# Attention and a four-expert MoE in float32: the first expert product in three float32r passes, the second without its seven-product scheme

## The chip, the cores and the metric

The kernel runs on one NeuronCore of one Trainium2 chip. Its time is what the device needs for one execution, in microseconds; the figure given is the median of the runs. A profile is one execution, recorded by the hardware; its span goes from the first to the last instruction.

The engines by their names in the profile: PE is TensorE (matmuls), PEld its weight loads, ACT is ScalarE, DVE is VectorE, POOL is GpSimd, SP issues the DMAs. Each takes its instructions in the order in which they were put down, and waits for semaphores of the others.

## The reference

Polynomial-sketch attention on inputs of 4 batches x 4 heads x 1088 tokens x 32, whose output, 4352 tokens of 128 numbers, is the input `x` of a mixture of four experts:

```python
p = domain_probs / (domain_probs.sum(-1, keepdims=True) + 1e-09)   # (4352, 4)
out = np.zeros((N, D), dtype=np.float32)                           # (4352, 128)
for e in range(E):                                                 # 4 experts
    h = np.maximum(x @ w1[e], 0.0)                                 # w1[e]: (128, 1024)
    out += p[:, e:e + 1] * (h @ w2[e])                             # w2[e]: (1024, 128)
return out.astype(np.float32)
```

All of it is float32. The two expert products are nearly all of the arithmetic.

## The kernel before, in words

The tokens, transposed so that the 128 features are the partitions (`xT`), are cut into eleven chunks of 128, 448, six times 512, 320, 256 and 128 columns (`CHUNKS`). The first and the last chunk are "plain" and are done with tokens as output partitions. Every chunk goes through `NQ` = 16 steps: 4 experts `e` times 4 pairs of 128-wide blocks of the hidden layer (`f`), two blocks `j` in each step. The main loop walks `i` over all steps of all chunks and calls `first(i, work)`, then `second(i - LA)` with `LA` = 2: the second product runs two steps behind the first.

- `first`, before: for each block `j` a float32 product of 128x128 weights with the chunk's columns, issued by `both` as two column halves of 64 (`on_side` alternates them, line 202), into a bank of pool `ps_h`. ScalarE rectifies it into `hid` (line 817), and VectorE's `rectify_and_subtract` (line 786) makes the combinations of half chunks that the seven-product scheme needs.
- `second`, before: seven products of 64 output rows and half a chunk's columns in place of eight, with weights from `w2_sb` and from their sums `w2s` (made once on GpSimd by `weight_sums`), accumulated over the expert's four steps in two banks, `o0` and `o1`, with one buffer each.
- `gather(m, e)`, after an expert's last `second`: two ScalarE copies of the accumulators into `ev` (lines 920 and 921), then, in the generator `gather_rest`, sums on GpSimd, two copies that move 64 partitions (933, 934), the multiplication with the gates and the sum over the experts in `total`. `turn_back` transposes the total and stores it.
- `work` issues pieces of the attention of later tokens (`front`: `keys`, `queries`, `attend`) between these steps, as many as the coming chunks need; all of the attention's matmuls are 64 columns wide (`on_side`).
- SP carries every load and store in one queue: batches of q, k, v (`load_batch`), the gates (`store_gates`, `load_gate`), the way of the attention's output through DRAM (`xd`) into `xT`, and the output.

The order on each engine is the order in which these Python calls put instructions down (`manual_schedule`). PSUM has eight banks of 512 float32 columns; before, three belong to `ps_h`, two to `ps_o`, one to `ps_f`, two to `ps_n`.

What follows an expert's last second product, before (in `gather`, an ordinary function, called in the main loop):

```python
nc.scalar.copy(_ap(ev, 0, P, 0, [[2 * w, 2], [1, w]]), _ap(a0, 0, P, 0, two))
nc.scalar.copy(_ap(ev, 0, P, w, [[2 * w, 2], [1, w]]), _ap(a1, 0, P, 0, two))
...
return gather_rest(m, e, ev, yz)
```

and the loop's end, which the change leaves as it is:

```python
second(i - LA)
mm, kk = steps[i - LA]
if kk % NP == NP - 1 and not plain(mm):
    ending = chain(ending, gather(mm, kk // NP))
else:
    next(ending, None)
```

Of the kernel before, what the change touches and what calls it, by code (L numbers as in the profile page):

```python
# [9 lines left out]
BF16 = mybir.dt.bfloat16  # L10
I32 = mybir.dt.int32
# [12 lines left out]
def kernel(  # L24
# [52 lines left out]
    ps_h = ctx.enter_context(tc.tile_pool(name="ps_h", bufs=3, space=bass.MemoryType.PSUM))  # L77
# [10 lines left out]
    def load_rows(src, b, name, part=slice(0, S)):  # L88

        d = kn if name == "kn" else qn  # L90
        if b not in d:
            d[b] = lpool.tile([P, S], F32, tag=name, bufs=2, name=name)
        c, n = part.start, part.stop - part.start
        base = src.offset + b * H * S * D
        if name == "qn" and b == B - 1:
            for c, n, t in ((0, (G - 4) * D, 0), ((G - 4) * D, 4 * D, S - P)):
                nc.sync.dma_start(d[b][:, c : c + n], bass.AP(src.tensor, base + t * D, [[S * D, H], [n, 32], [1, n]]))
        else:
            nc.sync.dma_start(d[b][:, part], bass.AP(src.tensor, base + c, [[G * D, P], [1, n]]))
# [163 lines left out]
    gates = dram.tile([B, GE * 32], F32, name="gates")  # L263
# [28 lines left out]
    def store_gates():  # L292
        nc.vector.transpose(pt[:, :], pn[:, :])
        for b in range(B):
            nc.sync.dma_start(
                gates[b].rearrange("(x r j) -> r x j", r=32, j=32),
                pt[32 * b : 32 * b + 32, :].rearrange("r (x j) -> r x j", j=32),
            )
# [11 lines left out]
    def load_gate(m, engine=nc.sync):  # L310
        gate[m] = mpool.tile([P, CW * E], F32, tag="gate", name="gate")
        for b, c, n, at in parts(m):
            engine.dma_start(
                gate[m][:, at * E : (at + n) * E], gates[b, c * E : (c + n) * E].partition_broadcast(P)
            )
# [342 lines left out]
    w2s = cpool.tile([P, E, FB // 2, 4, HP], F32, name="w2s")  # L658

    def block(e, i, j):  # L660
        return _ap(w2_sb, 0, P, e * FB * DM + P * j + HP * i, [[2 * DM, FB // 2], [1, HP]])

    def weight_sums(e):
        s = [w2s[:, e, :, i, :] for i in range(4)]
        for out, in0, in1, op in (
            (s[0], block(e, 1, 0), block(e, 1, 1), ALU.add),
            (s[1], s[0], block(e, 0, 0), ALU.subtract),
            (s[2], block(e, 0, 0), block(e, 1, 0), ALU.subtract),
            (s[3], block(e, 0, 1), s[1], ALU.subtract),
        ):  # L670
            nc.gpsimd.tensor_tensor(out=out, in0=in0, in1=in1, op=op)
            yield

    def start():
# [9 lines left out]
        for gi in range(3):  # L684
            kf.append(psum(ps_h, "h"))
# [7 lines left out]
        fq = [psum(ps_o, "o0"), psum(ps_o, "o1"), psum(ps_n, "num")]  # L693
# [26 lines left out]
        qT = apool.tile([P, QW], F32, tag="qT2", name="qT2")  # L720
# [7 lines left out]
        early[b, n] = psum(ps_o, "o1")  # L728
# [26 lines left out]
    def gate_of(m, e):  # L755
        return _ap(gate[m], 0, P, 32 * e, [[32 * E, CHUNKS[m] // 32], [1, 32]])

    def by_blocks(t, n, off=0):
        return _ap(t, 0, P, off, [[32, n // 32], [1, 32]])

# [14 lines left out]
    def first(i, work):  # L775
# [5 lines left out]
        w = n // 2  # L781
        hd = mpool.tile([P, 4 * CW], F32, tag="hid", bufs=4, name="hid")
        hid[i] = hd

        def rectify_and_subtract(out, src, in1):
            nc.vector.scalar_tensor_tensor(out=out, in0=src, scalar=0.0, in1=in1, op0=ALU.max, op1=ALU.subtract)  # L786

        if plain(m):
            if i in begun_hp:
# [22 lines left out]
            return  # L812
        for j in range(2):
            hp = psum(ps_h, "h")
            c = P * (2 * f + j)
            both(hp[:, 0:n], w1_sb[:, e, c : c + P], xT[:, START[m] : START[m] + n], start=True, stop=True)
            nc.scalar.activation(hd[:, n * j : n * j + n], hp[:, 0:n], ACTF.Relu)  # L817
            if j == 0:
                rectify_and_subtract(hd[:, 4 * w : 5 * w], hp[:, w:n], hd[:, 0:w])
            else:  # L820
                rectify_and_subtract(
                    _ap(hd, 0, P, 5 * w, [[w, 2], [1, w]]),
                    _ap(hp, 0, P, w, [[0, 2], [1, w]]),
                    _ap(hd, 0, P, w, [[3 * w, 2], [1, w]]),
                )
                rectify_and_subtract(hd[:, 7 * w : 8 * w], hp[:, 0:w], hd[:, 6 * w : 7 * w])
            work()

    begun = [0, 0]

    def second(i):
# [3 lines left out]
        if plain(m):  # L835

            if f == 0:
                acc[m] = psum(ps_o, f"o{e % 2}")
# [24 lines left out]
        if f == 0:  # L863
            acc[m, e] = [psum(ps_o, "o0"), psum(ps_o, "o1")]
            begun[:] = [0, 0]
        w = n // 2
        blk = lambda a, j: w2_sb[:, e, 2 * f + j, HP * a : HP * a + HP]
        new = lambda a: w2s[:, e, f, a, :]
        place = lambda a: hd[:, w * a : w * a + w]

        todo = (
            [(blk(0, 0), place(0)), (new(3), place(3)), (blk(0, 1), place(2)), (new(1), place(6))],
            [(new(2), place(5)), (new(0), place(4)), (blk(1, 1), place(7)), (new(1), place(6))],
        )
        at = [0, 0]
        for _ in range(7):
            s = turn[0]
            p = at[s]
            at[s] += 1

            fresh = p >= begun[s]
            begun[s] = max(begun[s], p + 1)
            wt, mv = todo[s][p]
            on_side(
                lambda s: acc[m, e][p // 2][half[s], w * (p % 2) : w * (p % 2) + w],
                lambda s: wt,
                lambda s: mv,
                start=(fresh and p % 2 == 0),
                stop=(f == NP - 1),
                skip_group_check=True,  # L890
            )

    def turn_back(m, src):

        n = CHUNKS[m]
        ob = mpool.tile([P, CW], F32, tag="ob", name="ob")
# [12 lines left out]
    def gather(m, e):  # L909

        n = CHUNKS[m]
        w = n // 2
        a0, a1 = acc.pop((m, e))
        ev = mpool.tile([P, 2 * CW], F32, tag="ev", name="ev")
        two = [[w, 2], [1, w]]
        add = lambda out, in0, in1, op=ALU.add: nc.gpsimd.tensor_tensor(out=out, in0=in0, in1=in1, op=op)  # L918

        nc.scalar.copy(_ap(ev, 0, P, 0, [[2 * w, 2], [1, w]]), _ap(a0, 0, P, 0, two))  # L920
        nc.scalar.copy(_ap(ev, 0, P, w, [[2 * w, 2], [1, w]]), _ap(a1, 0, P, 0, two))  # L921
        yz = mpool.tile([P, 2, CW // 2], F32, tag="yz", bufs=1, name="yz")
        add(yz[:, :, 0:w], _ap(ev, 0, P, 0, [[2 * w, 2], [1, w]]), _ap(ev, 0, P, 3 * w, [[0, 2], [1, w]]))
        return gather_rest(m, e, ev, yz)

    def gather_rest(m, e, ev, yz):
        n = CHUNKS[m]
        w = n // 2
        two = [[w, 2], [1, w]]
        add = lambda out, in0, in1, op=ALU.add: nc.gpsimd.tensor_tensor(out=out, in0=in0, in1=in1, op=op)  # L930
        yield
        sh = mpool.tile([P, CW // 2], F32, tag="sh", bufs=1, name="sh")
        nc.scalar.copy(sh[HP:P, 0:w], yz[0:HP, 0, 0:w])  # L933
        nc.scalar.copy(sh[0:HP, 0:w], yz[HP:P, 1, 0:w])
        add(ev[HP:P, 0:w], yz[HP:P, 0, 0:w], sh[HP:P, 0:w])
        add(ev[0:HP, 2 * w : 3 * w], yz[0:HP, 1, 0:w], sh[0:HP, 0:w])
        ct = mpool.tile([P, CW], F32, tag="ct", bufs=1, name="ct")
        add(_ap(ct, 0, P, 0, two), _ap(ev, 0, P, 0, [[0, 2], [1, w]]), _ap(ev, 0, P, w, two))
        if e == 0:
            total[m] = mpool.tile([P, CW], F32, tag="total", name="total")  # L940
        add(by_blocks(ct if e else total[m], n), by_blocks(ct, n), gate_of(m, e), ALU.mult)
        if e:
            add(total[m][:, 0:n], total[m][:, 0:n], ct[:, 0:n])
# [9 lines left out]
    behind = cpool.tile([P, 1], F32, name="behind")  # L953
# [17 lines left out]
    for i in range(3):  # L971
        begun_hp[i] = psum(ps_h, "h")
        half_columns(i, begun_hp[i], 0)
    to_sum = chain.from_iterable(weight_sums(e) for e in range(E))
    ending = iter(())
    for i in range(len(steps) + LA):
        if i < len(steps):
# [16 lines left out]
            if i > NQ - 4:  # L994
                if i == NQ - 3:

                    nc.gpsimd.tensor_copy(behind[:, :], xT[:, START[2] - 1 : START[2]])
                next(to_sum, None)
            if i == 2:
                gate_quotients()  # L1000
            elif i == 5:
                store_gates()
                load_gate(1)
                load_gate(2)
                load_batch(1)
            if m > 1 and kq == LA + 3 and m + 2 < NC:
                load_gate(m + 1)
# [41 lines left out]
```

## Time and profile before

| | |
|---|---|
| median of 3 runs | 488.05 us (487.61 to 488.38) |
| span of the profiled execution | 485.9 us |
| median less span (what lies around it) | 2.15 us |
| PE busy | 481.5 us, 99% |
| DVE busy | 320.9 us, 66% |
| ACT busy | 246.8 us, 51% |
| POOL busy | 230.0 us, 47% |
| granted TensorE clock | 1.000 |

No other time of the profiled execution is recorded; the span is what the parts are summed against.

How to read the views: a group's line gives the source line, engine, operation, tiles (out<-in), shape (partitions x elements) and count, then the busy time in us, the mean of one in ns, the idle time of the engine before them, and what ended it. A float32 matmul is two records of PE, each with a weight load. A chain line gives start, length, engine, tile and line, and how many records were merged. A wait line reads "engine tile line <- who released it: us in total, times, longest".

### The profile page before, as it was taken

How to read it: one execution, taken by the hardware profiler on the slowest of the kernel's cores; microseconds unless marked ns; L12 is line 12 of the kernel's file. 1: busy time of each engine (PE TensorE's matmuls, PEld its weight loads, DVE VectorE, ACT ScalarE, POOL GpSimd, SP SyncE). 2: the span in 40 equal slices, each digit the busy share in tenths (PEclk: the TensorE clock that was granted, in tenths of full speed). 3: DMA queues.
4: the chain of work that ended last, by engine and by line, in shares of the span. 5: the costliest groups of instructions: out<-in, count | busy, mean ns of one | idle time of the engine just before them, and what ended most of it. 6: DMA issues, size and time to landing. Idle time of an engine off the chain costs nothing.

```text
span 485.9 us, 11377 instructions
## 1 busy us (share of the span) xinstructions
PE 481.5 (99%) x4551; PEld 362.7 (75%) x4551; DVE 320.9 (66%) x759; ACT 246.8 (51%) x496; POOL 230.0 (47%) x270
## 2 busy tenths in 40 slices
PE   8999999999999999999999999999999999999997
PEld 6965666667777777777777777677777777999997
DVE  6859675686766668486776757668684666665642
ACT  4354564445544555355445555445455555566651
POOL 5172654435444455415455444424555445555571
PEclk9999999999999999999999999999999999999999
DMA  7990050211003123031103100021101200120001
GB/s 223 278 299 10 23 150 12 88 20 45 2 9 106 24 69 93 2 89 20 40 1 130 24 12 1 3 86 24 34 0 56 50 1 0 45 55 4 15 1 20
DMA packets 37772, 26.25 MB, mean 54 GB/s; under 512 B 24824, under 2 KB 34520, under 8 KB 37208
## 3 DMA queue, kind: packets, MB, share of 16 engines
q1 hardware_dynamic: 37704, 25.53, 18.9%
q8 instruction: 36, 0.59, 0.5%
q14 instruction: 16, 0.13, 0.1%
q10 hardware_dynamic: 16, 0.00, 0.0%
HBM read 21.28 MB, written 4.24 MB: 53 GB/s over the span
## 4 chain that ended last, share of the span: by engine, by line
PE 97%; DMA 1%; DVE 1%; issue 0%; SPq 0%; ACT 0%; ACTq 0%
PE h L202 50%; PE o L202 41%; PE f L202 3%; PE den L202 2%; DMA kn<-in_k_dram 1%; PE num L202 1%; DVE qp L501 0%; DVE kp L391 0%; DVE kT L328 0%; DVE qT L488 0%; SPq L125 0%; DVE end L856 0%; DVE kvz L414 0%; ACT fs L360 0%; ACT vx L337 0%
## 5 line engine op out<-in xcount | busy, mean ns | idle before, releaser
L202 PE MATMUL h<-xT,w_sb 128*64 128x512 f32 (+5 forms) x1424 | 300.2, 491 | 0.0
L786 DVE SCALAR_TENSOR_TENSOR hid<-h,hid 128x256 f32<-128x256 f32 (+6 forms) x432 | 203.7, 472 | 143.3 <-ACT hid L817 134.9
L817 ACT ACTIVATE hid<-h 128x512 f32<-128x512 f32 (+3 forms) x288 | 158.5, 550 | 192.3 <-PE h L202 146.2
L202 PE MATMUL o<-hid,w2s 128*64 128x256 f32 (+3 forms) x1152 | 224.0, 355 | 0.0
L202 PEld LDWEIGHTS h<-xT,w_sb 128*64 128x64 f32 x1424 | 147.5, 137 | 50.4 <-issue 6.4
L202 PE MATMUL o<-hid,w_sb 128*64 128x256 f32 (+3 forms) x864 | 183.7, 355 | 0.0
L202 PEld LDWEIGHTS o<-hid,w2s 128*64 128x64 f32 x1152 | 132.2, 137 | 28.9
L930 POOL TENSOR_TENSOR ev<-yz,sh 64x256 f32<-64x256 f32 (+3 forms) x72 | 48.7, 676 | 159.9 <-ACT sh L933 157.2
L202 PEld LDWEIGHTS o<-hid,w_sb 128*64 128x64 f32 x864 | 100.5, 137 | 25.2 <-issue 5.8
L918 POOL TENSOR_TENSOR yz<-ev 128x512 f32<-128x512 f32 (+3 forms) x36 | 41.7, 1160 | 60.4 <-ACT ev L921 60.2
L930 POOL TENSOR_TENSOR ct<-ev 128x512 f32<-128x512 f32 (+3 forms) x36 | 42.5, 1182 | 2.8
L930 POOL TENSOR_TENSOR total<-total,ct 128x512 f32<-128x512 f32 (+3 forms) x27 | 31.9, 1181 | 2.1
L930 POOL TENSOR_TENSOR ct<-ct,gate 128x512 f32<-128x512 f32 (+3 forms) x27 | 31.8, 1177 | 2.1
L501 DVE TENSOR_TENSOR qp<-qa,qb 64x512 f32<-64x512 f32 (+5 forms) x44 | 30.1, 685 | 1.0
L920 ACT COPY ev<-o 128x512 f32<-128x512 f32 (+3 forms) x36 | 19.4, 539 | 12.7 <-PE o L202 12.3
L202 PE MATMUL o<-w_sb,hid 128*64 128x128 f32 x256 | 22.3, 273 | 0.0
L921 ACT COPY ev<-o 128x512 f32<-128x512 f32 (+3 forms) x36 | 19.4, 539 | 2.0
L202 PEld LDWEIGHTS o<-w_sb,hid 128*64 128x64 f32 x256 | 18.1, 137 | 1.6 <-issue 0.9
L809 ACT ACTIVATE hid<-h 128x256 f32<-128x256 f32 x23 | 8.4, 384 | 18.3 <-PE h L202 17.9
L391 DVE TENSOR_TENSOR kp<-fs 128x256 f32<-128x256 f32 (+1 forms) x24 | 16.6, 696 | 0.1
L933 ACT COPY sh<-yz 64x256 f32<-64x256 f32 (+3 forms) x36 | 13.7, 380 | 1.7 <-POOL yz L918 0.8
L202 PEld LDWEIGHTS den<-kvx,qp 128*64 128x64 f32 x240 | 12.5, 137 | 2.5 <-issue 0.5
(129 smaller groups left out, 247.5 us busy)
## 6 DMA issues: line engine op xcount, KB each, us to landing
w_sb<-in_moe_w_dram SPq DMA_DIRECT2D x8, 512.0 KB, 5.8
gate<-gates SPq DMA_DIRECT2D x4, 1024.0 KB, 4.7
kn<-in_k_dram SPq DMA_DIRECT2D x4, 544.0 KB, 7.0
vn<-in_v_dram SPq DMA_DIRECT2D x16, 128.0 KB, 3.5
gate<-gates SPq DMA_DIRECT2D x2, 896.0 KB, 6.4
qn<-in_q_dram SPq DMA_DIRECT2D x2, 544.0 KB, 4.0
out_dram<-ob SPq DMA_DIRECT2D x16, 64.0 KB, 2.0
qn<-in_q_dram SPq DMA_DIRECT2D x2, 480.0 KB, 5.0
```

The lines of the kernel that those rows point to most:

```text
L202: nc.tensor.matmul(out(s), weights(s), moving(s), **flags)
L391: eng.tensor_tensor(out=_ap(kps[b], 0, P, 256 * t0 + P * p + 64 * x, [[256, n], [32, 2], [R, 4], [1, R]]), in0=_ap(src, 0, P, off + 4 * x, ...
L501: nc.vector.tensor_tensor(out=qp[p][64 * x : 64 * x + 64, 0:n], in0=qa[64 * p : 64 * p + 64, 0:n], in1=qb[64 * p : 64 * p + 64, 0:n], op=A ...
L786: nc.vector.scalar_tensor_tensor(out=out, in0=src, scalar=0.0, in1=in1, op0=ALU.max, op1=ALU.subtract)
L809: nc.scalar.activation(hd[:, 0 : 2 * n], hp[:, 0 : 2 * n], ACTF.Relu)
L817: nc.scalar.activation(hd[:, n * j : n * j + n], hp[:, 0:n], ACTF.Relu)
L918: add = lambda out, in0, in1, op=ALU.add: nc.gpsimd.tensor_tensor(out=out, in0=in0, in1=in1, op=op)
L920: nc.scalar.copy(_ap(ev, 0, P, 0, [[2 * w, 2], [1, w]]), _ap(a0, 0, P, 0, two))
L921: nc.scalar.copy(_ap(ev, 0, P, w, [[2 * w, 2], [1, w]]), _ap(a1, 0, P, 0, two))
L930: add = lambda out, in0, in1, op=ALU.add: nc.gpsimd.tensor_tensor(out=out, in0=in0, in1=in1, op=op)
L933: nc.scalar.copy(sh[HP:P, 0:w], yz[0:HP, 0, 0:w])
```

## The change

`w1` and the tokens are cut into a high and a low piece of at most twelve bits each, scaled, with the difference of the two as a third: `wa`, `wb`, `wd` for the weights (ScalarE and VectorE, `weight_parts`, one piece of work per step from step 7 on), `xa`, `xb`, `xd` for the tokens (`token_parts`, at the last step of the chunk before). The product is then `wa xa + wb xb` in one bank and `wd xd` in another, as float32r matmuls on full 128x128 tiles; ScalarE copies the first out with a scale, VectorE subtracts the second from it, ScalarE rectifies the result in place, one block later. The second product is a plain float32 product on full tiles into one bank. `gather` has one copy and no sums over halves. The gates lie in DRAM by expert and are loaded by expert, in tiles of one chunk's columns.

The diff, cut to its core:

```diff
-    ps_h = ctx.enter_context(tc.tile_pool(name="ps_h", bufs=3, space=bass.MemoryType.PSUM))
+    ps_h = ctx.enter_context(tc.tile_pool(name="ps_h", bufs=2, space=bass.MemoryType.PSUM))
+    ps_g = ctx.enter_context(tc.tile_pool(name="ps_g", bufs=2, space=bass.MemoryType.PSUM))
     ps_o = ctx.enter_context(tc.tile_pool(name="ps_o", bufs=1, space=bass.MemoryType.PSUM))
...
+    def weight_parts(e):
+        HF = F // 2
+        for c in (slice(0, HF), slice(HF, F)):
+            nc.scalar.activation(wa[:, e, c], w1_sb[:, e, c], ACTF.Copy, scale=4096.0 * NEAR)
+            stt(wb[:, e, c], w1_sb[:, e, c], 4096.0, wa[:, e, c].bitcast(F32), ALU.subtract)
+            yield
+            stt(wd[:, e, c], wa[:, e, c].bitcast(F32), R12, wb[:, e, c].bitcast(F32), ALU.subtract)
+            yield
...
+    def token_parts(m):
...
+        nc.scalar.activation(xa[:, 0:n], x, ACTF.Copy, scale=R12 * NEAR)
+        stt(xb[:, 0:n], xa[:, 0:n].bitcast(F32), -4096.0, x, ALU.add)
+        nc.vector.tensor_tensor(
+            out=xd_[:, 0:n], in0=xa[:, 0:n].bitcast(F32), in1=xb[:, 0:n].bitcast(F32), op=ALU.subtract
+        )
...
         for j in range(2):                                   # in first()
-            hp = psum(ps_h, "h")
-            both(hp[:, 0:n], w1_sb[:, e, c : c + P], xT[:, START[m] : START[m] + n], start=True, stop=True)
-            nc.scalar.activation(hd[:, n * j : n * j + n], hp[:, 0:n], ACTF.Relu)
...
+            g1, g2 = psum(ps_h, "h"), psum(ps_g, "g")
+            nc.tensor.matmul(g1[:, 0:n], wa[:, e, c], xa, start=True, stop=False)
+            nc.tensor.matmul(g1[:, 0:n], wb[:, e, c], xb, start=False, stop=True)
+            nc.tensor.matmul(g2[:, 0:n], wd[:, e, c], xd_, start=True, stop=True)
+            out = hd[:, n * j : n * j + n]
+            nc.scalar.activation(out, g1[:, 0:n], ACTF.Copy, scale=1.0 + R12)
+            rectify()
+            nc.vector.tensor_tensor(out=out, in0=out, in1=g2[:, 0:n], op=ALU.subtract)
+            to_rectify.append(out)
             work()
...
+    def rectify():
+        while to_rectify:
+            out = to_rectify.pop(0)
+            nc.scalar.activation(out, out, ACTF.Relu)
...
         if f == 0:                                           # in second()
-            acc[m, e] = [psum(ps_o, "o0"), psum(ps_o, "o1")]
...
+            acc[m, e] = psum(ps_o, "o")
+        for j in range(2):
+            nc.tensor.matmul(
+                acc[m, e][:, 0:n],
+                w2_sb[:, e, 2 * f + j, :],
+                hd[:, n * j : n * j + n],
+                start=(f == j == 0),
+                stop=(f == NP - 1 and j == 1),
+            )
...
     def gather(m, e):
         n = CHUNKS[m]
...
-        return gather_rest(m, e, ev, yz)
...
+        ev = mpool.tile([P, CW], F32, tag="ev", bufs=1, name="ev")
+        nc.scalar.copy(ev[:, 0:n], acc.pop((m, e))[:, 0:n])
+        g = gate.pop((m, e))[:, 0:n]
         if e == 0:
             total[m] = mpool.tile([P, CW], F32, tag="total", name="total")
+            nc.gpsimd.tensor_tensor(out=total[m][:, 0:n], in0=ev[:, 0:n], in1=g, op=ALU.mult)
+        else:
+            nc.gpsimd.tensor_tensor(out=ev[:, 0:n], in0=ev[:, 0:n], in1=g, op=ALU.mult)
+            nc.gpsimd.tensor_tensor(out=total[m][:, 0:n], in0=total[m][:, 0:n], in1=ev[:, 0:n], op=ALU.add)
         yield
...
             first(i, work)                                   # in the main loop
-            if i > NQ - 4:
...
+            if i > NQ - 10:
+                next(to_part, None)
+            if kq == NQ - 1 and m + 2 < NC:
+                while have[0] < START[m + 1] + CHUNKS[m + 1]:
+                    piece()
+                token_parts(m + 1)
```

In the changed kernel's line numbers: `weight_parts` 679 with `stt` 673, `token_parts` 692 and 694, the three matmuls 833 to 835, the copy 837, the subtraction 839, the rectification 848, the second product 885, the copy in `gather` 913.

More of the change, by code (lines that the diff above doesn't have):

```diff
@@ L10 @@
 BF16 = mybir.dt.bfloat16
+F32R = mybir.dt.float32r
 I32 = mybir.dt.int32
@@ L91, in load_rows @@
         if b not in d:
-            d[b] = lpool.tile([P, S], F32, tag=name, bufs=2, name=name)
+            d[b] = lpool.tile([P, S], F32, tag=name, bufs=1 if name == "kn" else 2, name=name)
         c, n = part.start, part.stop - part.start
@@ L260 @@
     mask_a = [[4 * x + l // R for l in range(32)] for x in range(2)]
-    gates = dram.tile([B, GE * 32], F32, name="gates")
+    gates = dram.tile([B, E, GE * 32 // E], F32, name="gates")
     pn = cpool.tile([P, GE], F32, name="pn")
@@ L294, in store_gates @@
         for b in range(B):
[L295 to L298, printed above, removed]
+            for e in range(E):
+                p = list(pt.ap)[0][0]
+                nc.sync.dma_start(
+                    gates[b, e].rearrange("(x r j) -> r x j", r=32 // E, j=32),
+                    bass.AP(pt.tensor, pt.offset + (32 * b + e) * p, [[E * p, 32 // E], [32, GE // 32], [1, 32]]),
+                )
     def parts(m):
@@ L308, with load_gates @@
     gate = {}
[L310 to L315, printed above, removed]
+    def load_gates(m, experts):
+        for e in experts:
+            gate[m, e] = mpool.tile([P, CW], F32, tag="gate", bufs=6, name="gate")
+            for b, c, n, at in parts(m):
+                nc.sync.dma_start(gate[m, e][:, at : at + n], gates[b, e, c : c + n].partition_broadcast(P))
     xT = cpool.tile([P, B * S], F32, name="xT")
@@ L655, in queries, with stt @@
         yield from attend(b, c, n, qp)
[L658 to L671, printed above, removed]
-            yield
+    R12 = 2.0 ** -12
+    NEAR = 1.0 - 2.0 ** -13
+    wa = cpool.tile([P, E, F], F32R, name="wa")
+    wb = cpool.tile([P, E, F], F32R, name="wb")
+    wd = cpool.tile([P, E, F], F32R, name="wd")
+    def stt(out, in0, scalar, in1, op1):
+        nc.vector.scalar_tensor_tensor(out=out, in0=in0, scalar=scalar, in1=in1, op0=ALU.mult, op1=op1)
+    def weight_parts(e):
[3 more added lines that the diff above has]
+            stt(wb[:, e, c], w1_sb[:, e, c], 4096.0, wa[:, e, c].bitcast(F32), ALU.subtract)
+            yield
+            stt(wd[:, e, c], wa[:, e, c].bitcast(F32), R12, wb[:, e, c].bitcast(F32), ALU.subtract)
+            yield
+    xparts = {}
+    def token_parts(m):
+        n = CHUNKS[m]
+        xa, xb, xd_ = (mpool.tile([P, CW], F32R, tag=f"x{i}", name=f"x{i}") for i in "abd")
+        x = xT[:, START[m] : START[m] + n]
+        nc.scalar.activation(xa[:, 0:n], x, ACTF.Copy, scale=R12 * NEAR)
[3 more added lines that the diff above has]
+        )
+        xparts[m] = xa, xb, xd_
     def start():
@@ L684, in start @@
         for gi in range(3):
-            kf.append(psum(ps_h, "h"))
+            kf.append(psum(ps_h, "h") if gi < 2 else psum(ps_g, "g"))
         value = value_copy(b)
@@ L692, in start @@
             pass
-        fq = [psum(ps_o, "o0"), psum(ps_o, "o1"), psum(ps_n, "num")]
+        fq = [psum(ps_o, "o"), psum(ps_g, "g"), psum(ps_n, "num")]
         for i in range(3):
@@ L719, in start @@
         n1 = UNITS[b][1]
-        qT = apool.tile([P, QW], F32, tag="qT2", name="qT2")
+        qT = apool.tile([P, QW], F32, tag="y", name="qT2")
         turns = query_turns(b, n, n1, qT)
@@ L727, in start @@
         next(first)
-        early[b, n] = psum(ps_o, "o1")
+        early[b, n] = psum(ps_g, "g")
         both(early[b, n][:, 0:n1], sq[:, :], qT[:, 0:n1], start=True, stop=True)
@@ L753, in plain @@
         return m in (0, NC - 1)
[L755 to L759, printed above, removed]
     begun_hp, made_hp = {}, {}
@@ L780, in first @@
         n, (e, f) = CHUNKS[m], divmod(kq, NP)
-        w = n // 2
-        hd = mpool.tile([P, 4 * CW], F32, tag="hid", bufs=4, name="hid")
+        hd = mpool.tile([P, 2 * CW], F32, tag="hid", bufs=3, name="hid")
         hid[i] = hd
-        def rectify_and_subtract(out, src, in1):
-            nc.vector.scalar_tensor_tensor(out=out, in0=src, scalar=0.0, in1=in1, op0=ALU.max, op1=ALU.subtract)
         if plain(m):
+            rectify()
             if i in begun_hp:
@@ L812, in first @@
             return
+        xa, xb, xd_ = (x[:, 0:n] for x in xparts[m])
         for j in range(2):
-            hp = psum(ps_h, "h")
-            c = P * (2 * f + j)
-            both(hp[:, 0:n], w1_sb[:, e, c : c + P], xT[:, START[m] : START[m] + n], start=True, stop=True)
[L817 to L826, printed above, removed]
-            work()
-    begun = [0, 0]
+            c = slice(P * (2 * f + j), P * (2 * f + j + 1))
+            g1, g2 = psum(ps_h, "h"), psum(ps_g, "g")
[4 more added lines that the diff above has]
+            nc.scalar.activation(out, g1[:, 0:n], ACTF.Copy, scale=1.0 + R12)
+            rectify()
+            nc.vector.tensor_tensor(out=out, in0=out, in1=g2[:, 0:n], op=ALU.subtract)
+            to_rectify.append(out)
+            work()
+    to_rectify = []
+    def rectify():
+        while to_rectify:
+            out = to_rectify.pop(0)
+            nc.scalar.activation(out, out, ACTF.Relu)
     def second(i):
@@ L837, in second @@
             if f == 0:
-                acc[m] = psum(ps_o, f"o{e % 2}")
+                acc[m] = psum(ps_g, "g") if e % 2 else psum(ps_o, "o")
             for j in range(2):
@@ L863, in second @@
         if f == 0:
-            acc[m, e] = [psum(ps_o, "o0"), psum(ps_o, "o1")]
[L865 to L890, printed above, removed]
+            acc[m, e] = psum(ps_o, "o")
[6 more added lines that the diff above has]
+                stop=(f == NP - 1 and j == 1),
             )
@@ L895, in turn_back @@
         n = CHUNKS[m]
-        ob = mpool.tile([P, CW], F32, tag="ob", name="ob")
+        ob = mpool.tile([P, CW], F32, tag="ob", bufs=1, name="ob")
         nc.vector.transpose(ob[:, 0:n], src)
@@ L913, in gather @@
         n = CHUNKS[m]
[L914 to L923, printed above, removed]
-        return gather_rest(m, e, ev, yz)
[L926 to L938, printed above, removed]
+        ev = mpool.tile([P, CW], F32, tag="ev", bufs=1, name="ev")
+        nc.scalar.copy(ev[:, 0:n], acc.pop((m, e))[:, 0:n])
+        g = gate.pop((m, e))[:, 0:n]
         if e == 0:
             total[m] = mpool.tile([P, CW], F32, tag="total", name="total")
-        add(by_blocks(ct if e else total[m], n), by_blocks(ct, n), gate_of(m, e), ALU.mult)
-        if e:
-            add(total[m][:, 0:n], total[m][:, 0:n], ct[:, 0:n])
+            nc.gpsimd.tensor_tensor(out=total[m][:, 0:n], in0=ev[:, 0:n], in1=g, op=ALU.mult)
+        else:
+            nc.gpsimd.tensor_tensor(out=ev[:, 0:n], in0=ev[:, 0:n], in1=g, op=ALU.mult)
+            nc.gpsimd.tensor_tensor(out=total[m][:, 0:n], in0=total[m][:, 0:n], in1=ev[:, 0:n], op=ALU.add)
         yield
@@ L951, in gather_rest @@
             turn_back(m, total.pop(m)[:, 0:n])
-    behind = cpool.tile([P, 1], F32, name="behind")
     start()
@@ L971 @@
     for i in range(3):
-        begun_hp[i] = psum(ps_h, "h")
+        begun_hp[i] = psum(ps_h, "h") if i < 2 else psum(ps_g, "g")
         half_columns(i, begun_hp[i], 0)
-    to_sum = chain.from_iterable(weight_sums(e) for e in range(E))
+    to_part = chain.from_iterable(weight_parts(e) for e in range(E))
     ending = iter(())
@@ L993 @@
             first(i, work)
-            if i > NQ - 4:
-                if i == NQ - 3:
-                    nc.gpsimd.tensor_copy(behind[:, :], xT[:, START[2] - 1 : START[2]])
-                next(to_sum, None)
+            if i > NQ - 10:
[4 more added lines that the diff above has]
+                token_parts(m + 1)
             if i == 2:
@@ L1002 @@
                 store_gates()
-                load_gate(1)
-                load_gate(2)
+                load_gates(1, range(E))
                 load_batch(1)
-            if m > 1 and kq == LA + 3 and m + 2 < NC:
-                load_gate(m + 1)
+            if m and m + 2 < NC and kq in (LA + 3, NQ - 4):
+                load_gates(m + 1, range(2) if kq == LA + 3 else range(2, E))
         if i == LA:
```

## The prediction

> **What bounds the kernel now.** I read the page's busy times and chain first, then the groups by shape, then the chain in order of time over two steps.
>
> ```profile
> span 485.9 us, 11377 instructions
> PE 481.5 (99%) x4551; PEld 362.7 (75%) x4551; DVE 320.9 (66%) x759; ACT 246.8 (51%) x496; POOL 230.0 (47%) x270
> PE 97%; DMA 1%; DVE 1%; issue 0%; SPq 0%; ACT 0%; ACTq 0%
> ```
>
> TensorE is busy for the whole span and is nearly the whole chain: nothing makes it wait. The chain over two steps of a 512-column chunk:
>
> ```profile
> 253.13 1.89 PE h L202 x8
> 255.03 1.51 PE o L202 x13
> 256.54 1.72 PE h L202 x8
> 258.25 1.33 PE o L202 x13
> ```
>
> A first product is eight records in 1.72 us (two column halves run beside each other, so 0.215 per record); a step repeats after (259.59 - 253.13) / 2 = 3.23 us, so the second product, fourteen records, takes 1.51. A plain fp32 product of 128x128 by 512 columns is thus 0.86 us. The waits and groups by shape show the other side:
>
> ```profile
> ACT hid L817 <- PE h L202: 146.2, 199, 2.9
> L817 ACT ACTIVATE hid<-h 128x512 f32<-128x512 f32 x192 | 114.8, 598 | 150.8 <-PE h L202 118.7 <-ACT sh L934 14.2 <-issue 5.8
> L920 ACT COPY ev<-o 128x512 f32<-128x512 f32 x24 | 14.1, 586 | 9.1 <-PE o L202 9.1
> L934 ACT COPY sh<-yz 64x256 f32<-64x256 f32 x24 | 9.7, 405 | 0.6
> L817 ACT ACTIVATE hid<-h 128x256 f32<-128x256 f32 x32 | 12.3, 384 | 8.1 <-DVE hid L786 4.8 <-PE h L202 2.2 <-ACT sh L934 0.6
> L786 DVE SCALAR_TENSOR_TENSOR hid<-h,hid 128x512 f32<-128x512 f32 x96 | 65.9, 686 | 26.2 <-ACT hid L817 25.1
> L639 DVE TENSOR_TENSOR qf<-f,qf 128x512 f32<-128x512 f32 x3 | 2.0, 680 | 0.0
> ```
>
> ScalarE waits for TensorE, never the reverse: it has slack today. Its instruction costs 0.60 us at 512 columns, some 0.02 more when it reads SBUF (405 against 384 ns at 256), and the next one follows 0.02 later (0.6 us idle before 24 of L934). VectorE takes 0.69 us for 512 columns.
>
> **Part by part, TensorE's own work.** The chunks that change hold 4096 columns: 16 steps on 8 chunks' worth of 512, so 128 wide steps. First product: six float32r matmuls. No row shows float32r. An fp32 product is four times 0.215; bounds are 0.215 (one column per cycle, a quarter of it) and 0.86 (no cheaper than fp32). I take 0.215, because pieces cut to twelve bits are made for one pass each, and it is the pace of the existing records. Then 6 x 0.215 = 1.29 against 1.72: 128 x 0.43 = -55. Second product without the seven-product scheme: 2 x 0.86 = 1.72 against 1.51: 128 x 0.21 = +27. Together -28.
>
> Weight loads on 128x128 tiles: the trace has only 64-column fp32 loads (137 ns) and 128-column bf16 ones (136 ns), all beside running matmuls; even the 66-column matmuls of the attention come every 0.05 us (240 records in 11.5 us) with loads of 137 ns. I take them as hidden; the other end is the first rival.
>
> **The wait that it adds: one accumulator bank.** Before, gather was a plain function: its two copies out of o0/o1 stood on ScalarE right after the expert's last second product. Now gather is itself a generator, so its copy (L913) is put down only at the next(ending) of the following step, after that step's first() and the next second(). In the built order ScalarE has: copy j0, rectify the old j1, copy j1, rectify j0, then the ev copy; and the next expert's first matmul (L885) waits for that copy, since "o" has one buffer. Queued behind it on TensorE is everything. From the start of that step's first(): g1 is complete at 0.43, its tail and hand-over are some 0.20 (a 512-column record lasts 0.592, its stream 0.43, and VectorE started 0.03 us after ScalarE in the timeline); then 0.598 + 0.618 + 0.598 + 0.618 + 0.586 and four gaps of 0.024 and a hand-over of 0.04: 3.78. TensorE is through with first() at 1.29, so it waits 2.49 us. For n columns the same sum gives 1.21 + 0.0025 n: 2.33 at 448, 2.01 at 320, 1.85 at 256. There are 24 such ends at 512, 3 at 448, 4 at 320, 4 at 256: 59.8 + 7.0 + 8.0 + 7.4 = +82. It is the largest term. VectorE's subtract (0.69 after copy j0) is done before the second rectify, so it does not lengthen this chain. Bounds: 70 if the hand-overs are nothing, 95 if attention's copies on ScalarE stand in half of the chains.
>
> **Chunk starts.** token_parts stands after first() of a chunk's last step. ScalarE's four instructions end at 3.14 after that step's start, xa (0.618) at 3.78, VectorE's xb at 4.50 and xd at 5.19; TensorE is ready at 1.29 + 1.72 = 3.01 and uses them in turn, the last at 5.23 instead of 3.44: 1.8 us. Six chunks of 512 at 1.8, the others at 1.1 to 1.5: +15 (0 to 20).
>
> **Smaller terms.** Two g banks are freed by VectorE, which also carries attention (its 0.69 us pieces stand ahead of a subtract): +5, between 0 and 12. Weight pieces: eight on ScalarE, sixteen on VectorE at 0.69; nine of these fall into the 128-column chunk, where VectorE is 73 to 96% busy (windows view, 16 to 24 us) and the next chunk's attention hangs on it: +2, between 0 and 4, the cover gone only there. ScalarE grows by 288 rectifications, some 165 us, less 33 of gather's copies, to about 390 of 567: no bound by its sum, 2.5 in a 3.0 us step. POOL loses w2s and most of gather, nothing waited for it: 0; SP gets twelve more gate stores and about thirty more gate loads, all a chunk ahead of use: 0, and 2 at most for batch 1's loads that stand behind them.
>
> Full tiles now alternate with attention's 64-column tiles, 77 changes in the built order. No row of the trace shows such a change among fp32 matmuls. If each waits for the tail of the last matmul (0.592 - 0.43 = 0.165), the bound is 13, and below it 0 where the change falls into a wait; I take +5. The Trainium skill, page "TensorEngine Tiling", section "Key Properties", speaks against the change here: it says that changing the tiling mode drains the array. By that rule the term would be nearer to 13 and the sum 577; the sum below does not use it.
>
> The granted clock is 1.00 over the whole span, with no idle TensorE. The waits above leave it idle for 2.5 us out of every 14.5. The Trainium skill, "TensorE: Matmul & The Clock Gate", section "Why this matters for your kernels", wants no idle gap over about 3 us, else the clock halves: these gaps stay below it, so the rule too adds nothing. If it failed, an estimate from that page's 3 us would be 35 x 1.5 = 52 us and a sum of 621; no trace here shows such a gap.
>
> **Sum.** 485.9 - 28 + 82 + 15 + 5 + 2 + 5 = 567 us of span. The median of the runs stands 488.05 - 485.9 = 2.15 above the span of the profiled execution: 569.
>
> **Rivals.** (1) Weight loads show. Six float32r and four fp32 loads per step, 0.137 each or a part of it: up to 128 x 1.37 = 175 more, less some 20 that the longer first() takes from the accumulator wait: 590 to 725. For it: no full-tile fp32 load in the trace; against: all loads there are hidden. Chance 0.10. (2) float32r streams at half pace, 0.43, as one fp32 record on one half does: first() 2.58, +165; copy j1 then starts at 2.35 and the wait falls to 1.66 each, -27: 707. Chance 0.08. (3) The change does not do what it says: a float32r matmul costs 0.86 like fp32. First() 5.16, +495, waits halved, -42: about 1020. Chance 0.02. (4) Not slower: the accumulator is free in time. If the ev copy ran right after the expert's last matmul (0.20 + 0.586 + 0.04 = 0.83, less than 1.29), there is no wait, and 569 - 82 = 487, or 482 if tile changes cost nothing. It decides from 0.06 us per end on: 35 x 0.06 = 2 us more than that and the kernel is slower. Against it: the order of ScalarE's queue, and the wait that L885 carries. Chance 0.03.
>
> **How the numbers follow.** My forecast, 569, has 0.77, with its own range 550 to 595 (terms at their bounds, not all on one side). 0.2% is about what a measurement of this kernel tells from no change. Only rival 4 is not slower: 0.02 faster, 0.01 same, 0.97 slower. The range from 550 to 640 takes in the forecast's own and the lower half of rival 1; left out are rivals 2, 3, 4, the upper half of 1 and a few hundredths of the forecast's tails.
>
> **What would show it.** After the change: idle TensorE before L885 of about 2.5 us, 35 times, ended by ScalarE's L913; idle before L833 to L835 at the nine chunk starts, ended by L692 and L673/L694; float32r records every 0.215 us; plain fp32 records every 0.43 on a full tile; POOL down to about 85 us, ScalarE up to 390. Wrong would be: records of float32r at 0.43 or more, loads between matmuls with TensorE idle "for issue", or L885 not waiting. If the clock falls below full after the gaps, the sum is too low.

## The result, and the profile after

| | before | after |
|---|---|---|
| median of the runs, us | 488.17 (487.61 to 488.38, 4 runs) | 582.13 (576.76 to 590.76, 4 runs) |
| ratio | | 1.189 (95%: 1.1834 to 1.1945) |
| span of the profiled execution, us | 485.9 | 581.6 (its time 583.37) |
| granted TensorE clock in it | 1.000 | 0.979 |

The change costs 19%. Forecast were 569 us and a range of 550 to 640: the time lies in the range, 13 us above the number. The run at 590.76, over 1.5% above the fastest, is left out of the ratio. The other three differ in their clock, and span times clock is nearly the same for all: 581.6 x 0.979 = 569.4, 575.0 x 0.991 = 569.8, 579.0 x 0.982 = 568.6. So about 569 us is, by estimate, the span at a full clock, and 5 to 12 us of each of the three go to the clock. The forecast of the span, without any loss of clock, was 567.

The page of the changed kernel: span, busy times, the clock in 40 slices, the chain by engine.

```profile
span 581.6 us, 8014 instructions
PE 507.9 (87%) x2823; PEld 320.4 (55%) x2823; DVE 308.6 (53%) x649; ACT 328.0 (56%) x693; POOL 85.4 (15%) x109
...
PEclk9998999999998999999999898889999999999999
...
PE 73%; ACT 15%; DVE 8%; issue 2%; DMA 1%; POOL 0%; ACTq 0%; SPq 0%; DVEq 0%
```

TensorE fell from 99% to 87% of a longer span, and from 97% to 73% of the chain. ScalarE, which had nothing in the chain before, has 15% of it, at only 56% busy. The clock row has 8 in places where it was full before. The waits of the changed kernel (engine, tile, line, who released it: us in total, times, longest):

```profile
PEld o L885 <- ACT ev L913: 68.9, 35, 3.5
...
PEld h L833 <- ACT xa L692: 9.2, 9, 2.2
...
PEld h L834 <- DVE xb L673: 7.3, 9, 1.1
...
PEld g L835 <- DVE xd L694: 4.3, 9, 0.5
```

Line 885, the second product, waits 35 times for the one copy out of the accumulator (L913): four experts in each of nine chunks, less the first. The other three are the nine chunk starts. One such wait, in the chain in order of time (start, us, what):

```profile
310.66 0.86 PE o L885 x2
311.52 0.23 PE h L833
311.75 0.24 PE h L834
312.00 0.02 issue
312.02 0.02 ACTq L837
312.03 0.04 issue
312.08 0.60 ACT hid L837
312.68 0.52 ACT hid L848
313.20 0.49 ACT hid L837
313.68 0.52 ACT hid L848
314.20 0.49 ACT ev L913
314.69 0.04 issue
314.73 1.55 PE o L885 x3
```

This is the chain of the prediction, link by link: the first half of first(), then copy, rectify, copy, rectify and the ev copy on ScalarE, and only then the second product. TensorE beside it (the bracket is idle time and its releaser):

```profile
311.59 0.39 PE L834 MATMUL h<-xb,wb 128*128 128x512 f32 x1
311.82 0.40 PE L835 MATMUL g<-xd,wd 128*128 128x512 f32 x1
312.06 0.39 PE L833 MATMUL h<-xa,wa 128*128 128x512 f32 x1
312.29 0.40 PE L834 MATMUL h<-xb,wb 128*128 128x512 f32 x1
312.52 0.40 PE L835 MATMUL g<-xd,wd 128*128 128x512 f32 x1
314.73 1.12 PE L885 MATMUL o<-hid,w_sb 128*128 128x512 f32 x2 [1.81 <-ACT ev L913]
```

A float32r matmul starts every 0.23 us, and its record lasts 0.40. A record's last 0.165 us are tail, and the first record after a wait is 0.10 us longer than one in the stream (0.49 to 0.51 in place of 0.39 at 512 columns for L833 to L835), so the stream of matmuls stands still longer than the bracket says: 2.08 us here and at most of the 512-column ends. Added up over the trace so, in stretches above 0.06 us, TensorE's idle time is 3.1 us before and 103 after: 66 in the 35 waits before L885, 16.5 at the nine chunk starts, 12 in changes between full and 64-column tiles (38 each way), 8.5 in other places.

### The profile page after: what moved, and what is told of

The parts are those of the page before. It is cut to its first block, busy times and chain, and to the rows that moved or that the text cites. A ratio compares the mean times of both kernels' runs of the same rounds, so it can differ in the third digit from the quotient of the medians.

```text
span 581.6 us, 8014 instructions
## 1 busy us (share of the span) xinstructions
PE 507.9 (87%) x2823; PEld 320.4 (55%) x2823; DVE 308.6 (53%) x649; ACT 328.0 (56%) x693; POOL 85.4 (15%) x109
## 4 chain that ended last, share of the span: by engine, by line
PE 73%; ACT 15%; DVE 8%; issue 2%; DMA 1%; POOL 0%; ACTq 0%; SPq 0%; DVEq 0%
PE o L885 39%; PE h L833 9%; PE h L834 9%; PE g L835 8%; ACT hid L837 6%; ACT hid L848 5%; PE f L204 3%; ACT ev L913 3%; PE den L204 2%; PE h L204 2%; DVE hid L839 1%; DVE qp L504 1%; DVE xd L694 1%; DVE xb L673 1%; PE g L204 1%
## 5 line engine op out<-in xcount | busy, mean ns | idle before, releaser
L839 DVE TENSOR_TENSOR hid<-hid,g 128x512 f32<-128x512 f32 (+3 forms) x288 | 180.3, 626 | 248.1 <-PE h L834 121.4
L885 PE MATMUL o<-hid,w_sb 128*128 128x512 f32 (+3 forms) x576 | 258.0, 572 | 56.3 <-ACT ev L913 56.3
L837 ACT ACTIVATE hid<-h 128x512 f32<-128x512 f32 (+3 forms) x288 | 157.5, 547 | 219.6 <-PE h L834 218.1
L885 PEld LDWEIGHTS o<-hid,w_sb 128*128 128x128 f32 x576 | 105.9, 193 | 136.2 <-ACT ev L913 68.9
L848 ACT ACTIVATE hid<-hid 128x512 f32<-128x512 f32 (+3 forms) x288 | 166.5, 578 | 1.2 <-DVE hid L839 1.2
L833 PE MATMUL h<-xa,wa 128*128 128x512 f32 (+3 forms) x288 | 160.5, 557 | 2.8 <-ACT xa L692 2.4
L834 PE MATMUL h<-xb,wb 128*128 128x512 f32 (+3 forms) x288 | 107.7, 374 | 4.8 <-DVE xb L673 4.7
L835 PE MATMUL g<-xd,wd 128*128 128x512 f32 (+3 forms) x288 | 108.3, 376 | 2.9 <-DVE xd L694 1.6
L833 PEld LDWEIGHTS h<-xa,wa 128*128 128x128 f32 x288 | 55.7, 193 | 44.5 <-issue 22.4
L834 PEld LDWEIGHTS h<-xb,wb 128*128 128x128 f32 x288 | 55.3, 192 | 38.8 <-issue 26.1
L835 PEld LDWEIGHTS g<-xd,wd 128*128 128x128 f32 x288 | 54.5, 189 | 15.6 <-DVE xd L694 4.3
L920 POOL TENSOR_TENSOR total<-total,ev 128x512 f32<-128x512 f32 (+3 forms) x27 | 31.4, 1164 | 2.1
L204 PE MATMUL h<-xT,w_sb 128*64 128x128 f32 (+1 forms) x256 | 18.5, 268 | 1.9 <-ACT hid L825 1.9
L913 ACT COPY ev<-o 128x512 f32<-128x512 f32 (+3 forms) x36 | 19.2, 534 | 0.0
L204 PEld LDWEIGHTS h<-xT,w_sb 128*64 128x64 f32 x256 | 14.1, 137 | 3.8 <-ACT hid L825 2.1
```

The lines of the kernel that those rows point to most:

```text
L204: nc.tensor.matmul(out(s), weights(s), moving(s), **flags)
L833: nc.tensor.matmul(g1[:, 0:n], wa[:, e, c], xa, start=True, stop=False)
L834: nc.tensor.matmul(g1[:, 0:n], wb[:, e, c], xb, start=False, stop=True)
L835: nc.tensor.matmul(g2[:, 0:n], wd[:, e, c], xd_, start=True, stop=True)
L837: nc.scalar.activation(out, g1[:, 0:n], ACTF.Copy, scale=1.0 + R12)
L839: nc.vector.tensor_tensor(out=out, in0=out, in1=g2[:, 0:n], op=ALU.subtract)
```

## Experiments

All times beside the kernel before, whose runs took 487.3 to 488.6 us; the edits are against the changed kernel where nothing else is said.

**The copy at once.** `gather` becomes an ordinary function that copies and returns a generator, as it was before the change.

```diff
         nc.scalar.copy(ev[:, 0:n], acc.pop((m, e))[:, 0:n])
+        return gather_rest(m, e, ev)
+
+    def gather_rest(m, e, ev):
+        n = CHUNKS[m]
         g = gate.pop((m, e))[:, 0:n]
```

> The changed kernel with gather an ordinary function again: its one copy out of the accumulator is put down right after the expert's last second product, the rest stays a generator. Theory (the copy stands too late in ScalarE's queue, and the idle gaps also halve the clock): the idle stream time before the second product, 70 us over the expert ends, goes to under 5, the clock record goes from 0.979 to above 0.995, together 582 - 68 - 11 = about 503 us (497 to 509). Rival A (ScalarE as a whole is too slow with its 288 added rectifications): the wait only moves to another place, 560 to 582. Rival B (what is lost lies in changes of tile shape and weight loads): 575 to 582, idle before the second product unchanged in sum.

Measured: 509.37 us (508.87 to 512.62), ratio 1.0448 (1.0413 to 1.0483), span 507.1, clock 1.000; just above the expected 497 to 509. Its waits:

```profile
PEld h L833 <- ACT xa L692: 9.2, 9, 2.2
...
PEld o L885 <- ACT ev L913: 0.2, 1, 0.2
```

The 68.9 us became 0.2, the wait at the chunk starts stayed as it was to the tenth, and the clock was full (0.990 to 1.000 over the four runs). Three lines of code hold 73 of the 94 us: some 62 are the wait (569 at full clock against 507; idle stream 103 against 40), the rest is the clock.

**The copy at once for every second expert.** If each wait costs by itself, half of them should cost half.

```diff
+        if e % 2:
+            nc.scalar.copy(ev[:, 0:n], acc.pop((m, e))[:, 0:n])
+        return gather_rest(m, e, ev)
+
+    def gather_rest(m, e, ev):
+        if not e % 2:
+            nc.scalar.copy(ev[:, 0:n], acc.pop((m, e))[:, 0:n])
```

> The changed kernel with the copy put down at once for the odd experts alone; the even experts keep the late place. 18 of the 35 waits go. Theory: idle before the second product falls by half, 70 to about 35 us, and with it the number of halved clock windows (7 before) falls to 2 to 5: 582 - 35 - 5 = 542 us (534 to 550). Rival A: under 10 us less.

Measured: 547.54 us (544.02 to 551.73), ratio 1.1244 (1.1182 to 1.1307), clock 0.997 in the profiled run; within the expected 534 to 550.

```profile
PEld o L885 <- ACT ev L921: 38.0, 18, 3.5
```

Eighteen waits are left, of 2.11 us in the mean, and 35 of the 73 us are gone: each wait costs by itself.

**The tokens' pieces two steps earlier.** Takes away what the chunk starts wait for.

```diff
-            if kq == NQ - 1 and m + 2 < NC:
+            if kq == NQ - 3 and m + 2 < NC:
```

> The changed kernel with token_parts two steps earlier in the chunk before (step 13 of 16 instead of the last), nothing else. Theory: the idle time before the three float32r matmuls at the nine chunk starts, 17 us by stream time, goes below 5, so about 582 - 13 = 569 us, the rest unchanged and the clock still halved now and then (562 to 576). Rival A: VectorE and ScalarE are the limit, the pieces only push other work later: 578 to 585.

Measured: 578.84 us (575.42 to 581.95), ratio 1.1855 (1.1804 to 1.1907); span 576.7, clock 0.967.

```profile
PEld o L885 <- ACT ev L913: 73.1, 35, 5.1
...
PEld h L833 <- ACT xa L692: 0.5, 2, 0.2
```

A miss that taught something: the chunk-start waits are gone (9.2, 7.3 and 4.3 became 0.5, none and 0.4), and 576.7 x 0.967 = 557.7 at full clock is some 11 us less than 569, near the gain that was expected. But the profiled run has 11 windows of halved clock, of 3.413 us each, where the changed kernel has 7, and most of the gain went there. The time also lies where Rival A expected it, and in part as Rival A says: the wait before L885 grew from 68.9 to 73.1, with one of 5.1 us, where `xa` waits 3.5 us for its load in ScalarE's queue ahead of the ev copy.

**Both edits.**

> Both edits, the copy at once and token_parts two steps earlier. Theory: the two terms add up and the clock stays at 1.00: 582 - 68 - 13 - 12 = 489 us (482 to 495), TensorE idle under 15 us in the span, of the size of the kernel before. Rival A: 545 to 575. Rival B (shape changes and loads): not below 560.

Measured: 499.24 us (498.37 to 499.43), ratio 1.0223 (1.0208 to 1.0238), span 496.5, clock 1.000. Missed by 10 us. The steady step is right (TensorE, in the middle of a chunk, with nothing idle in it):

```profile
280.65 0.39 PE L834 MATMUL h<-xb,wb 128*128 128x512 f32 x1
280.88 0.39 PE L835 MATMUL g<-xd,wd 128*128 128x512 f32 x1
281.11 0.39 PE L833 MATMUL h<-xa,wa 128*128 128x512 f32 x1
281.34 0.40 PE L834 MATMUL h<-xb,wb 128*128 128x512 f32 x1
281.57 0.40 PE L835 MATMUL g<-xd,wd 128*128 128x512 f32 x1
281.81 1.88 PE L885 MATMUL o<-hid,w_sb 128*128 128x512 f32 x4
...
283.75 0.39 PE L834 MATMUL h<-xb,wb 128*128 128x512 f32 x1
```

From L834 of one step (280.65) to the next one's in the same place (283.75) it takes 3.11 us instead of 3.23: 1.39 for the six float32r matmuls (0.232 each) and 1.71 for the four records of fp32 (0.4285 each). That is a gain of 0.12 a step, 16 us in 128 steps, where the forecast had 28. The other part of the miss is idle time that the two edits do not touch: TensorE's stream still stands still for 29 us, 13 of them in changes of tile shape. The waits name some of the rest:

```profile
PEld g L835 <- DVE hid L839: 7.9, 12, 1.5
...
ACT xa L692 <- DMA xT<-xd: 4.1, 1, 4.1
...
PEld o L885 <- ACT ev L913: 3.2, 2, 3.0
```

These are VectorE's late subtracts, and one load of `xT` that comes too late for pieces made so early: `xa` stands in ScalarE's queue and holds up the ev copy behind it for 3 us.

**Both edits, tuned.** The tokens' pieces at `NQ - 2`, the weight pieces begun four steps later, attention kept further ahead.

```diff
-            if i > NQ - 10:
+            if i > NQ - 6:
-            if kq == NQ - 1 and m + 2 < NC:
+            if kq == NQ - 2 and m + 2 < NC:
-  ... (needed[c] + (8 if c > 1 else 4) - done[0]) ...
+  ... (needed[c] + (14 if c > 1 else 4) - done[0]) ...
```

> The kernel with the copy at once; token_parts one step earlier instead of two; the weight pieces start four steps later (step 11); the attention is asked for six pieces earlier. Theory: the 2.9 us wait for the xT load at one chunk start and part of the 4 us at the start of the 448-column chunk go: 499 - 4 = 495 us (491 to 498), still slower than the kernel before, because the steady step is 3.11 us against 3.23, which is worth 16 us, and TensorE idles some 18 us more than before and changes tile shape 77 times. Rival (the remaining loss is waits that better order can remove): below 488 us.

Measured: 496.41 us (495.21 to 498.12), ratio 1.0178 (1.0152 to 1.0204), span 493.9. That is within the expected 491 to 498; which of the three changes gained what was not tested apart. The best version with the new products that was run is still 1.8% slower than the kernel before.

**The second product alone.** The kernel before, its first product unchanged on half tiles (64 columns), with the plain second product on full tiles, into `o0` and `o1` by turns, one copy at once, no combinations, no `w2s`. This prices the second product and, since every step changes the tile shape twice, that change.

```diff
-            acc[m, e] = [psum(ps_o, "o0"), psum(ps_o, "o1")]
...
+            acc[m, e] = psum(ps_o, f"o{e % 2}")
+        for j in range(2):
+            nc.tensor.matmul(acc[m, e][:, 0:n], w2_sb[:, e, 2 * f + j, :], hd[:, n * j : n * j + n],
+                             start=(f == j == 0), stop=(f == NP - 1 and j == 1))
```

> The kernel before with the second part of the change alone: the second product as plain float32 on full 128x128 tiles into banks o0 and o1 by turns, gather with one copy put down at once, no combinations and no weight sums; the first product stays float32 in 64-column halves. Every step now changes the tile shape twice. Theory (a change to 64 columns costs 0.1 us, one back to 128 columns 0.2 us, as the changed kernel's trace shows around the attention's matmuls): 128 x (1.72 + 1.71 + 0.3 - 3.23) = +64, about 552 us (540 to 560). Rival (shape changes are free, only the arithmetic counts): 488 + 128 x 0.20 = 514 us (508 to 520).

Measured: 564.51 us (563.58 to 565.12), ratio 1.1567 (1.1547 to 1.1586), span 563.1, clock 1.000. TensorE in one step:

```profile
254.97 1.03 PE L202 MATMUL h<-xT,w_sb 128*64 128x512 f32 x4
255.93 1.99 PE L857 MATMUL o<-hid,w_sb 128*128 128x512 f32 x4
257.85 1.08 PE L202 MATMUL h<-xT,w_sb 128*64 128x512 f32 x4
```

The order of theories holds, the price was too low (expected were 540 to 560). Between the streams on both sides, by the records' ends, a change from 64 to 128 columns takes 0.20 us (0.09 idle and 0.105 until the first stream begins) and one from 128 to 64 takes 0.145. That is 0.345 for a pair: 144 pairs make 50 us, and with the second product's 26 the kernel should be 76 us slower; its span is 77 us longer (563.1 - 485.9).

**Fillers against the clock.** Six unread bf16 matmuls of 128x128 by 512 into a bank of `ps_h`, ahead of the second product that will wait; in the second kernel two in place of six. They add to the work and should bring time only by way of the clock.

```diff
         if i >= LA:
+            mm, kk = steps[i - LA]
+            if kk % NP == 0 and not plain(mm) and (kk or mm > 1):
+                wp = psum(ps_h, "h")
+                for _ in range(6):            # range(2) in the second kernel
+                    nc.tensor.matmul(wp[:, :], warm[:, 0:P], warm[:, :], start=True, stop=True)
             second(i - LA)
```

> The changed kernel, the copy still late, with six bfloat16 matmuls of 128x128 by 512 columns, whose result nothing reads, put on TensorE ahead of each expert's first second product, where TensorE waits for the copy. They take 6 x 0.22 = 1.3 of the 2.0 us gap and add nothing to the path. Theory (the clock is halved for one 3.41 us window after a window in which TensorE streamed nothing for some 2.1 us or more): no halved window within the span, granted clock 0.997 or more, 582 - 11 = 571 us (565 to 575). Rival (the halving comes from the float32r matmuls or the load of the other engines): clock still 0.97 to 0.99 and 578 to 588 us.

> As the kernel with six filling matmuls ahead of each expert's first second product, but with two: 0.44 of the gap of 2.08 us (at 512 columns) is filled, in front of it. Theory (what counts is the idle time within one free-running window of 3.41 us, with the limit at about 2.1 us): the longest usual idle stretch falls to 1.65, no window but the odd one is halved, clock 0.994 or more, 570 to 577 us, the same as with six. Rival (any gap of TensorE above a microsecond can halve the clock): clock 0.97 to 0.99, 577 to 585 us.

Measured: 574.86 us (573.31 to 577.15), ratio 1.1787 (1.1751 to 1.1823) with six, and 573.35 us (573.18 to 575.2), ratio 1.1763 (1.1742 to 1.1785) with two, both within what was expected. The spans and clocks of the two:

```profile
core 0: 571.9 us, clock 1.000
```

```profile
core 0: 573.4 us, clock 0.994
```

More matmuls, and 7 to 9 us less time: with 0.44 us of useless work (two at 0.218) in each wait the four runs have clocks of 0.994 to 0.997, with six 0.991 to 1.000, against 0.979 to 0.991 without. So the loss of clock is a cost of its own, and it shrinks when TensorE is idle for less of each wait.

**The late copy twice.** The opposite: the same copy made a second time lengthens each wait by half a microsecond.

```diff
+        nc.scalar.copy(ev[:, 0:n], acc[m, e][:, 0:n])
         nc.scalar.copy(ev[:, 0:n], acc.pop((m, e))[:, 0:n])
```

> The changed kernel with its late copy out of the accumulator made twice into the same tile, so that each of the 35 waits is longer by one ScalarE copy, 0.52 to 0.62 us: 18 to 22 us if only the wait counts, 600 to 604. Theory with the limit of 2.1 us of idle in a window: gaps of 2.6 us fall into one window with 2.1 or more in about half of the cases, so some 12 to 22 windows are halved in place of 6, clock 0.93 to 0.96, and the time 608 to 630. Rival (halving does not depend on the length of the gap): clock about 0.98 and 600 to 604 us.

Measured: 622.03 us (620.07 to 625.03), ratio 1.2747 (1.2692 to 1.2801); span 622.1.

```profile
core 0: 622.1 us, clock 0.945
```

```profile
PEld o L885 <- ACT ev L914: 88.9, 35, 4.1
```

The wait grew by 20.0 us, 0.57 each; the time by 40. At full clock the span would be 622.1 x 0.945 = 588, 18.5 above 569: the wait itself. The other half is the clock, with 20 halved stretches where there were 7. A further 0.57 us per wait costs twice its length. Time and number of halved stretches lie where they were expected.

## Why the prediction was right, and where it was off

**The mechanism** was the forecast's: the ev copy, put down a step late, holds the one accumulator bank. Removing the delay alone removed the 68.9 us of wait, and removing it for half of the experts removed half. Rival 4 (accumulator free in time) falls by the same line.

**The step that failed is the clock**, entered at 0: it cost 12 us in the profiled execution, nearly the whole distance between 569 and 582. The prediction took gaps below 3 us to be harmless, after the Trainium skill's page "TensorE: Matmul & The Clock Gate", section "Why this matters for your kernels", and wrote that if it failed the sum would be too low. Here it failed well below the page's 3 us: the runs show about 2.1 us of idle stream within one window of 3.41 us, and the measurement decides. The windows view of one wait, at its worst, and the two stretches behind it (us, busy of each engine, then the granted clock, DMA share, GB/s):

```profile
core 0: us, PE busy (x) PEld busy (x) DVE busy (x) ACT busy (x) POOL busy (x), PEclk, DMA share, GB/s
213.70:217.11 3.41, 0.49 (x3) 0.05 (x1) 1.91 (x4) 3.41 (x8) 0.00 (x0) 1.00 0.08 20
217.11:220.53 3.42, 3.30 (x5) 1.51 (x5) 0.13 (x1) 0.07 (x1) 2.53 (x2) 0.51 0.63 152
220.53:223.94 3.41, 3.41 (x11) 1.70 (x9) 1.88 (x4) 2.51 (x5) 0.00 (x0) 0.99 0.31 106
```

TensorE was busy for only 0.49 of 3.41 us, and in the next 3.41 us it ran at half the clock. The four records of L885 that fall there, beside four at full clock:

```profile
217.23 3.64 PE L885 MATMUL o<-hid,w_sb 128*128 128x512 f32 x4 [3.03 <-ACT ev L913]
314.73 1.98 PE L885 MATMUL o<-hid,w_sb 128*128 128x512 f32 x4 [1.81 <-ACT ev L913]
```

Every halved stretch inside this trace lasts 3.413 us, and all of them start on one fixed grid of that length. Seven windows are followed by a halved one. Two of them hold 3.2 and 2.5 us of idle stream, the other five 2.07 to 2.09. Four more windows hold 2.07 to 2.09 and are not followed by one. So the usual wait of 2.08 us stands on the edge, and there idle time alone does not say which window is followed; what else decides was not tested. Over the ten traces of the changed kernel and the experiments, every window inside the span with 2.12 us or more of idle stream is followed by a halved one, and none with 2.06 or less, but for one that was itself halved (with the earlier tokens, two halved windows in a row). What counts is the sum within one window and not one long gap: the window from 353.7 to 357.1 holds a chunk start, with 1.06 us of a wait for `xa`, 0.49 for `xb` and 0.51 for `xd`, and is followed by a halved one; so is one at the same chunk start in the kernel with two fillers (347.9 to 351.3). A further half microsecond per wait sends 20 windows over the edge.

**The first product** was mis-sized: six matmuls at 0.232 us each instead of 0.215, so -42 (128 x 0.33) where the sum has -55. By width the spacing is 0.119, 0.148, 0.203 and 0.232 us at 256, 320, 448 and 512 columns. The value 0.215 came from fp32 records on half tiles, which run in pairs. Rivals 2 and 3 (half pace, fp32's pace) fall.

**The second product** is right: 0.4285 a record, +26 for +27. The weight loads of 128 columns last 0.19 us (the groups have 193 ns) and hide under the stream: rival 1 falls, the steady step has no room for them.

**The accumulator wait**, +82 forecast, is 66 of idle stream (68.9 by the waits view): 2.08 at most of the 512-column ends, not 2.49. The groups by shape and ScalarE's timeline say why:

```profile
L848 ACT ACTIVATE hid<-hid 128x512 f32<-128x512 f32 x192 | 120.1, 625 | 0.0
...
L837 ACT ACTIVATE hid<-h 128x512 f32<-128x512 f32 x192 | 114.2, 595 | 171.2 <-PE h L834 169.7 <-PE g L835 1.3
...
312.08 0.60 ACT L837 ACTIVATE hid<-h 128x512 f32<-128x512 f32 x1 [1.55 <-PE h L834]
312.57 0.62 ACT L848 ACTIVATE hid<-hid 128x512 f32<-128x512 f32 x1
```

They last what the prediction took, 0.60 and 0.62, but they start, and in the chain above end, every 0.49 to 0.52 us: one begins 0.10 before the last has ended. The prediction added 0.02 between them, from two copies in a row (L933 and L934); there, before the change, 0.025 us do lie between, but not here. Five instructions take 2.62 instead of 3.11. The Trainium skill's page "ScalarE: Activation LUTs", section "What ACT_TABLE_LOAD costs", states an overlap of about 93 ns for ACTIVATEs in a row, and this trace agrees with 0.10. Some was given back: 0.26 us of hand-over to ScalarE instead of 0.20, 0.10 before the first stream of L885, and a first() that is 0.10 longer, which shortens the wait.

**ScalarE's sum** was put at 390 and is 328, for the most part for the same reason (its durations, overlaps counted twice, add up to 378); POOL's was put at 85 and is 85.4. **Chunk starts** had +15 and show 16.5 of idle stream. The **g banks** had +5 and show some 2 before L835; what the weight pieces' +2 came to, no run shows. **Tile changes** had +5 under a bound of 13: 38 changes to 64-column tiles show 0.14 to 0.15 us of idle stream each, and 34 of the 38 back to full tiles 0.20; four fall into waits. That is 12 us, the prices of the experiment on the second product. The bound was the better value, as the tiling rule that the prediction set aside had it.

**The sum remade** with the measured terms: 485.9 - 42 + 26 + (103 - 3) of idle = 570, beside the estimate of 569 at full clock, and 582 with 12 of clock; the span is 581.6. For the kernel with both edits it is 485.9 - 16 + (29 - 3) = 496, and the span is 496.5. So there the new products gain 16 us, and 26 more of idle stream, half of it in tile changes, lose them again. That the forecast of 567 lies so near to 569 is in part luck: the wait was 16 too long, the first product 13 too cheap, the tile changes 7 too cheap.

## What to carry to other kernels

Turning a function into a generator moved one copy by a step on its engine's queue, and with one accumulator bank that was worth more than all the arithmetic: for each bank with a single buffer, look up where in its engine's order the instruction stands that frees it, and what stands ahead. A chain across engines is summed from start-to-start distances rather than from durations. Idle time of TensorE has a second price: count it per window of the clock, and keep well below the edge, be it with a matmul that nobody reads.

## What the runs showed of the hardware

- The clock has a fixed grid of 3.413 us windows, and after a window with about 2.1 us or more of idle TensorE stream it is halved for the next one: always from 2.12 us on, never (from a window at full clock) at 2.06 or less, at times in between. A wait of 2.08 us is enough to stand on the edge; two bf16 matmuls of 0.218 us in each wait restore 0.994 to 0.997.
- Float32r on a full tile starts every 0.232 us at 512 columns, bf16 every 0.218, each of fp32's two records every 0.4285.
- Going from 64-column to 128-column fp32 tiles and back costs 0.345 us, 0.20 and 0.145, with the engine never without work: 50 us in a kernel that does it 144 times.
- On ScalarE an instruction can begin about 0.10 us before the preceding one ends: ACTIVATE after ACTIVATE (L837, L848), copy after ACTIVATE (L848, L913) and copy after copy (L340, L345 in the changed kernel). Other pairs leave 0.02 to 0.03 us between them: L920 and L921, L933 and L934, and an ACTIVATE and a copy (L817, L933) in the kernel before, and the copy made twice into one tile. So the kind of instruction does not decide; what does is not shown.
